# Seven-product steps: the first product's bank is copied into the fourth one's bank instead of being added afterwards

## The chip, the cores and the metric

The kernel runs on one core of one Trainium2 chip. What is measured is the device time of one execution in microseconds (us). The engines are TensorE (PE; its weight loads are listed as PEld), VectorE (DVE), ScalarE (ACT), GpSimd (POOL) and SyncE (SP), which issues most DMAs. A name such as L915 is a line of the kernel.

## The reference

Attention within chunks of 64 positions, and a gated feed-forward network on its result:

```python
scores = q_c @ k_c.T / sqrt(64)               # 8 batches, 8 heads, 9 chunks of 64, width 64
attn = softmax(scores)
x = (attn @ v_c) as (4608 tokens, 512)
g = x @ w_gate                                # 512 x 1536
out = (g * sigmoid(g)) * (x @ w_val) @ w_out  # 1536 x 512
```

All data are float32. The kernel splits each factor into an upper and a lower half in a shorter format and multiplies three pairs of halves, so every product below is made of three matmuls for each 128 rows of its inner dimension.

## The kernel before, in words

Tokens are worked on in batches of 512 (`N`), and the feed-forward network in twelve slices of 128 hidden columns (`f`, or a step). From slice 5 of the first batches on, gate and value of a slice are computed for two batches at once from seven products of half-size blocks in place of eight. Seven steps of this kind run in `first_seven` (L928; f = 5 to 11), and 36 in `gated_pair` (L1189), twelve for each of the three later pairs of batches (`both_steps`, L1256).

**A step.** Product i (`seventh`, L910 to L916; its matmuls are L915) takes six matmuls of 128x512 and adds into one of three PSUM banks. Bank `ps1` is from the pool `ps_a`; `ps2` and `ps3` are the two banks of the pool `ps_gv`. The order on TensorE is:

- products 0, 1 and 2 go to `ps1`, `ps2` and, added to what is there, `ps1`; after each of the first three ScalarE copies the bank to SBUF: the first copy (L953, L1202) to `h`, the second (L961, L1204) to `v2`, the third (L968, L1207) to `v1`;
- product 3 goes to `ps3`; VectorE adds it to `h` (`add`, L918; its instruction is L919), and ScalarE turns `h` into its Silu in place (L977, L1211);
- product 4 adds into `ps1`, and VectorE adds that bank to `v2`; product 5 adds into `ps2`, and VectorE adds that bank to `v1` and multiplies `h` by it (L555);
- product 6 adds into `ps1`, and ScalarE takes its Silu (L995, L1223), which VectorE multiplies by `v2`.

Between the products stand the four quarters (`turns`, L921) of the output projection of the step before: three matmuls each, L583 to L585 of 128x512 or L571 of 128x256. `parts` (L562) splits `h` for the next step's projection.

```python
seventh(ps1, pair.x, factors, 0, True)     # L1201
nc.scalar.copy(out=h, in_=ps1)             # L1202
...
seventh(ps3, pair.x, factors, 3, True)     # L1209
add(h, ps3)                                # L1210
nc.scalar.activation(h, h, AF.Silu, scale=2.0 ** -8)
```

**What else uses the banks.** `ps_gv` and `ps_a` also hold the attention's scores and outputs. In the steps 0, 3, 8 and 10 of a pair that is not the last, a burst of attention work for the next pair is put before the last quarter: `scores` (L1099) after steps 0 and 3, `cross` (L1118) after 8 and 10. In `scores` the second two banks of scores are in `ps_gv`; for each of them `less_top` (L318) takes a row maximum (L322) and subtracts it (L323) on VectorE. `cross` has its banks emptied by ScalarE (L398). The helpers `products` and `scores` (L292, L300) and `columns_crossed` (L386) write one bank with many 64x64 matmuls; in `products` and `columns_crossed` each of them has the flag `start`.

**What sets the order.** The order on TensorE, ScalarE and VectorE is the order of the program text throughout (L611). SyncE's is so until L1049 and GpSimd's from L1456 to L1559; in the pairs after that, from L1560, the order of those two is made when the program is built, from an estimated timeline. `load_weights` (L1181; its DMAs are L1186) loads the two tiles of factors of step i + 2 at the end of step i, into the place of step i's.

Of the kernel before, what the change touches and what calls it, by code (L numbers as in the profile page):

```python
# [13 lines left out]
AF = mybir.ActivationFunctionType  # L14
# [4 lines left out]
C = 64  # L19
# [14 lines left out]
def attn_then_gated_ffn(ctx: ExitStack, tc: tile.TileContext, qk, v, wgv, wo, out):  # L34
    nc = tc.nc
# [18 lines left out]
    def in_turn(x):  # L54

        return x.rearrange("p (a b) -> p b a", a=2)
# [158 lines left out]
    def save_w(f):  # L215
        kept_w[f] = store.tile([P, 2, 4 * Q], F32, name=f"w{f}")
        nc.sync.dma_start(out=kept_w[f], in_=w_both[f].bitcast(F32))
# [50 lines left out]
    class Attn:  # L268
# [23 lines left out]
        def products(self, tiles, pool=ps_a, tag="ps_a"):  # L292

            n = sum(t.shape[1] for t in tiles)
            ps = [pool.tile([P, n, T, C], F32, name="ps_a", tag=tag) for _ in range(2)]
            for i, t in enumerate(t[:, k] for t in tiles for k in range(t.shape[1])):
                self.scores(t, i, ps)
            return ps

        def scores(self, t, i, ps, first=None):  # L300
# [85 lines left out]
        def columns_crossed(self, v_t, p, n, pool=ps_a, tag="ps_a"):  # L386


            px = [pool.tile([P, n, T, C], F32, name="ps_a", tag=tag) for _ in range(2)]
            for i in range(n):  # L390
                for u in range(T):
                    for j in range(2):
                        for h in range(2):
                            r = (h ^ j) * C
                            nc.tensor.matmul(px[j][h * C:(h + 1) * C, i, u, :], v_t[i][r:r + C, j, u, :],  # L395
                                             self.turned[r:r + C, p + i, j, u, :], start=True, stop=True)
            for j in range(2):
                nc.scalar.copy(out=self.s[:, p:p + n, :, j], in_=px[j])  # L398

# [101 lines left out]
    def some(ps, a, f, g, which, first=True, last=True):  # L501
        for k, i in which:
            w = (w_hi, w_lo, w_hi)[i][f][:, g, k]
            x = a.x[k // 2][i == 0][:, k % 2]
            nc.tensor.matmul(ps, w, in_turn(x), start=first and (k, i) == which[0],  # L505
                             stop=last and (k, i) == which[-1])
# [12 lines left out]
    def save_o(f):  # L519
        nc.sync.dma_start(out=kept_o[f], in_=out_now[f].bitcast(F32))  # L520
        if f % 2 == 0:
            kept_raw.append(store.tile([P, 2, DM], F32, name=f"r{f}"))
        nc.sync.dma_start(out=kept_raw[f // 2][:, f % 2], in_=wo_raw[f])
# [14 lines left out]
    def product(a, f, g):  # L538
        ps = ps_gv.tile([P, N], F32, name="ps_gv")
        some(ps, a, f, g, IN_TURN)  # L540
        return ps
# [12 lines left out]
    def times(h, pv):  # L554
        nc.vector.scalar_tensor_tensor(out=h, in0=pv, scalar=2.0 ** -8, in1=h, op0=ALU.mult, op1=ALU.mult)  # L555

    def gated(a, f):
        h = gate(a, f)
        times(h, value(a, f))
        return h  # L560
# [57 lines left out]
    def put_off(h):  # L618
        f = len(waiting)
        if f % 2 == 0:  # L620
            kept_h.append(store.tile([P, 2, N], F32, name=f"h{f}"))
        waiting.append(kept_h[-1][:, f % 2])
        nc.scalar.dma_start(out=waiting[f], in_=h)
# [44 lines left out]
    class Product:  # L668
# [4 lines left out]
        def add(self, *which):  # L673
            for w in which:
                self.left -= 1
                some(self.ps, *self.at, [w], first=self.left == 3 * NK - 1, last=not self.left)
# [88 lines left out]
    for do in opening.split():  # L765
# [14 lines left out]
        else:  # L780
            b, i = int(do[1]), int(do[2])
# [128 lines left out]
    def seventh(ps, x, factors, i, first):  # L910
        which, q = FACTORS[i]
        w = [t.rearrange("p (i k m) -> p i k m", i=4, m=P)[:, q] for t in factors[which]]
        for k in range(NK // 2):
            for n, (u, v) in enumerate(((0, 1), (1, 0), (0, 0))):
                nc.tensor.matmul(ps, w[u][:, k], in_turn(x[i][v][:, k]), start=first and k == 0 and n == 0,  # L915
                                 stop=k == NK // 2 - 1 and n == 2, skip_group_check=True)  # L916
# [4 lines left out]
    def turns(which):  # L921

        if pending:
            project(*pending[0], which=which)
            if T - 1 in which:
                pending.pop()

    def first_seven(f, done, before, amid=None):  # L928

        o, w = down[f], up[f + 1] if f + 1 < NF else None  # L930
        if f + 2 < NF:
            up[f + 2].load()
        save_o(f - 1)
        done.save()
        if f == NF - 2:
            save_w(EARLY)
            save_w(EARLY + 1)
        factors = (w_both[f][:, 0], w_both[f][:, 1]), done.halves

        def product(ps, i, first):  # L940
            seventh(ps, x_first, factors, i, first)

        ps1 = ps_a.tile([P, N], F32, name="ps_a", tag="ps_a")
        ps2, ps3 = (ps_gv.tile([P, N], F32, name="ps_gv") for _ in range(2))
        h = hp.tile([P, N], F32, name="h")
        v1, v2 = (ld.tile([P, N], F32, name="v", tag="v_t") for _ in range(2))
        product(ps1, 0, True)
        if w:
            w.below()
            w.shift()  # L950
        if f + 1 < NF:
            down[f + 1].load()
        nc.scalar.copy(out=h, in_=ps1)  # L953
        o.below()
        if f < NF - 1:
            put_off(before)
        product(ps2, 1, True)
        if w:
            w.join()
            w.upper()  # L960
        nc.scalar.copy(out=v2, in_=ps2)  # L961
        turns([0])
        product(ps1, 2, False)
        quarters = Quarters(f + 1)
        if w:
            quarters.sums(w.t)
            w.lower()
        nc.scalar.copy(out=v1, in_=ps1)  # L968
        if w:
            quarters.upper()  # L970
        o.shift()
        o.join()
        product(ps3, 3, True)
        add(h, ps3)
        if w:
            quarters.lower()
        nc.scalar.activation(h, h, AF.Silu, scale=2.0 ** -8)  # L977
        turns([1])
        product(ps1, 4, False)
        add(v2, ps1)  # L980
        wo_f = out_weights(f, nc.gpsimd)
        product(ps2, 5, False)
        if f + 2 < NF:
            up[f + 2].scale()
        if f + 1 < NF:
            down[f + 1].scale()
        add(v1, ps2)
        times(h, v1)
        p = parts(a0, f, h)
        turns([2] if amid is None else [2, 3])  # L990
        if amid:
            amid()
        product(ps1, 6, False)
        h2 = const.tile([P, N], F32, name="h2", tag="ts") if f == NF - 2 else hp.tile([P, N], F32, name="h")
        nc.scalar.activation(h2, ps1, AF.Silu, scale=2.0 ** -8)  # L995
        if amid is None:
            turns([3])
        times(h2, v2)
        pending.append((p, wo_f))
        return quarters, h2  # L1000
# [188 lines left out]
    def gated_pair(pair, i, h, h2, inside, middle, beside):  # L1189

        def turn_of(t):
            if t in inside:
                turns([t])

        factors = loaded[STEPS[i]]
        ps1 = ps_a.tile([P, N], F32, name="ps_a", tag="ps_a")
        ps2 = ps_gv.tile([P, N], F32, name="ps_gv")
        ps3 = ps_gv.tile([P, N], F32, name="ps_gv")
        v12 = const.tile([P, 2, N], F32, name="v", tag=("ts", "wo1")[i % 2])
        v1, v2 = v12[:, 0], v12[:, 1]  # L1200
        seventh(ps1, pair.x, factors, 0, True)  # L1201
        nc.scalar.copy(out=h, in_=ps1)  # L1202
        seventh(ps2, pair.x, factors, 1, True)
        nc.scalar.copy(out=v2, in_=ps2)  # L1204
        turn_of(0)
        seventh(ps1, pair.x, factors, 2, False)
        nc.scalar.copy(out=v1, in_=ps1)  # L1207
        middle()
        seventh(ps3, pair.x, factors, 3, True)  # L1209
        add(h, ps3)  # L1210
        nc.scalar.activation(h, h, AF.Silu, scale=2.0 ** -8)  # L1211
        beside()
        turn_of(1)
        seventh(ps1, pair.x, factors, 4, False)
        add(v2, ps1)
        seventh(ps2, pair.x, factors, 5, False)
        add(v1, ps2)
        times(h, v1)
        if i == NF - 1:
            prepare_unit(pair, 0)  # L1220
        turn_of(2)
        seventh(ps1, pair.x, factors, 6, False)
        nc.scalar.activation(h2, ps1, AF.Silu, scale=2.0 ** -8)  # L1223
        times(h2, v2)
        turn_of(3)
        return parts(pair, i, h)
# [216 lines left out]
    a, pair = nxt, []  # L1443
# [29 lines left out]
    pair = pair[0]  # L1473
# [65 lines left out]
    for i in range(NF):  # L1539
        f = (i + EARLY) % NF  # L1540
        h = gated(a, f)
# [18 lines left out]
    for b in range(3, NB, 2):  # L1560
# [27 lines left out]
        if not pair.last:  # L1588
            pair = n
# [34 lines left out]
```

## Time and profile before

| | |
|---|---|
| median of 3 runs | 848.16 us |
| the three runs | 846.42, 848.16, 850.94 us |
| span of the profiled execution | 846.1 us |
| instructions | 16689 |
| TensorE busy | 828.3 us, 98% of the span |
| VectorE busy | 605.8 us, 72% |
| ScalarE busy | 433.5 us, 51% |
| GpSimd busy | 158.7 us, 19% |

The span is the time from the first to the last instruction of the profiled execution; the table of runs does not single that execution out, and the lowest of the three is 0.3 us above the span. A line of the timeline gives the start in us from the span's beginning, the duration in us, the engine, the line, the operation, what is written and read, and in brackets the idle time of the engine just before and what ended it. Successive matmuls overlap, so that the durations of single matmuls add up to more than the time they take together; starts are compared instead.

### The profile page before, as it was taken

The page shows a single profiled execution, that of the slowest core. Times are in us where ns is not written, and L with a number is a line of the kernel's source. Part 1 is how long each engine was busy: PE and PEld are TensorE (multiplying, and loading weights), DVE is VectorE, ACT ScalarE, POOL GpSimd, SP SyncE. Part 2 cuts the span into 40 slices and gives each one's busy share as a digit, 9 for nine tenths or more (in the row PEclk, how much of TensorE's full clock was granted, in tenths as well). Part 3 has the DMA queues.
Part 4 walks back from the last instruction along what each step waited for, and adds up shares of the span by engine and source line. Part 5 has one row for each costly group of instructions (what it writes and reads, how often), then busy time and mean ns, then how long its engine had stood idle before and what let it go on. Part 6 is the DMA issues. An engine that isn't in the chain of part 4 may idle for free.

```text
span 846.1 us, 16689 instructions
## 1 busy us (share of the span) xinstructions
PE 828.3 (98%) x6689; PEld 742.8 (88%) x6689; DVE 605.8 (72%) x946; ACT 433.5 (51%) x650; POOL 158.7 (19%) x118
## 2 busy tenths in 40 slices
PE   7999999999998999999999999999999999999997
PEld 6788888888887888888889998888889988888997
DVE  5898988863798965568886976688768943333475
ACT  5876889753525335535335744553337533333353
POOL 1300001102246641233110002313010002222100
PEclk9999999999999999999999999999999999999999
DMA  9698788899989999866678779656668576666643
GB/s 353 257 330 312 279 312 313 320 350 324 418 298 380 304 405 346 306 210 232 231 245 309 266 247 323 229 214 237 194 229 300 163 260 229 232 232 227 234 170 114
DMA packets 96654, 231.27 MB, mean 273 GB/s; under 512 B 32064, under 2 KB 58176, under 8 KB 83904
## 3 DMA queue, kind: packets, MB, share of 16 engines
q1 hardware_dynamic: 94848, 227.31, 75.1%
q10 hardware_dynamic: 1728, 2.88, 1.1%
q8 instruction: 53, 0.87, 0.4%
q14 instruction: 25, 0.20, 0.1%
HBM read 177.21 MB, written 52.95 MB: 272 GB/s over the span
## 4 chain that ended last, share of the span: by engine, by line
PE 86%; DMA 6%; DVE 3%; ACT 1%; SPq 1%; issue 1%; POOL 1%; DVEq 0%; POOLq 0%; ACTq 0%
PE ps_a L915 26%; PE ps_gv L915 19%; PE ps_o L571 14%; PE ps_gv L505 9%; PE ps_gv L571 6%; DMA v_t<-in_v 3%; PE ps_o L583 3%; PE ps_o L585 3%; PE ps_o L584 3%; DMA qk_t<-r 2%; PE ps_a L395 2%; PE ps_a L307 1%; DVE turned L382 1%; DMA both<-o 1%; DMA qk_t<-in_qk 1%
## 5 line engine op out<-in xcount | busy, mean ns | idle before, releaser
L915 PE MATMUL ps_a<-x,factors 128*128 128x512 f32 x864 | 210.7, 380 | 0.8 <-ACT v L1204 0.8
L915 PEld LDWEIGHTS ps_a<-x,factors 128*128 128x128 f32 x864 | 154.4, 190 | 18.1 <-issue 1.0
L915 PE MATMUL ps_gv<-x,factors 128*128 128x512 f32 x648 | 157.5, 379 | 0.1
L915 PEld LDWEIGHTS ps_gv<-x,factors 128*128 128x128 f32 x648 | 122.3, 189 | 17.9 <-PE ps_a L915 0.4
L1249 POOL TENSOR_TENSOR kept<-kept 128x512 f32<-128x512 f32 x39 | 56.9, 1459 | 365.3 <-DVE kept L555 361.0
L505 PE MATMUL ps_gv<-xh,w 128*128 128x512 f32 x352 | 103.4, 380 | 2.0 <-issue 2.0
L382 DVE STREAM_TRANSPOSE turned<-s_sb 32x256 f32<-32x256 f32 x192 | 83.7, 436 | 3.1
L70 ACT CAST hh<-kept 128x512 fp32r<-128x512 f32 x111 | 67.2, 617 | 28.8 <-PE ps_o L571 15.4
L505 PEld LDWEIGHTS ps_gv<-xh,w 128*128 128x128 f32 x352 | 66.4, 189 | 9.5 <-ACT xh L660 0.2
L1223 ACT ACTIVATE kept<-ps_a 128x512 f32<-128x512 f32 x36 | 21.5, 598 | 89.7 <-PE ps_a L915 89.3
L919 DVE TENSOR_TENSOR kept<-kept,ps_gv 128x512 f32<-128x512 f32 x30 | 20.6, 687 | 65.1 <-PE ps_gv L915 64.9
L71 DVE TENSOR_TENSOR hl<-kept,hh 128x512 fp32r<-128x512 f32 x84 | 57.2, 686 | 12.4 <-ACT hh L70 12.0
L505 PE MATMUL ps_gv<-xl,w 128*128 128x512 f32 x176 | 65.5, 382 | 0.0
L555 DVE SCALAR_TENSOR_TENSOR kept<-v,kept 128x512 f32<-128x512 f32 x66 | 45.7, 692 | 24.2 <-ACT kept L1223 18.0
L571 PE MATMUL ps_o<-sums,hh 128*128 128x256 f32 x504 | 62.7, 275 | 0.0
L571 PEld LDWEIGHTS ps_o<-sums,hh 128*128 128x128 f32 x504 | 59.3, 192 | 0.4 <-DVE hh L71 0.4
L571 PEld LDWEIGHTS ps_o<-both,hh 128*128 128x128 f32 x288 | 51.4, 189 | 6.8
L583 PE MATMUL ps_o<-both,hl 128*128 128x512 f32 x144 | 55.0, 382 | 0.8 <-DMA both<-o 0.8
L584 PE MATMUL ps_o<-both,hh 128*128 128x512 f32 x144 | 54.6, 379 | 0.0
L585 PE MATMUL ps_o<-both,hh 128*128 128x512 f32 x144 | 54.6, 379 | 0.0
L571 PE MATMUL ps_o<-both,hh 128*128 128x256 f32 x288 | 53.5, 276 | 0.0
L919 DVE TENSOR_TENSOR v<-v,ps_a 128x512 f32<-128x512 f32 x43 | 29.5, 686 | 22.0 <-PE ps_a L915 21.6
(164 smaller groups left out, 1442.4 us busy)
## 6 DMA issues: line engine op xcount, KB each, us to landing
factors<-w SPq DMA_DIRECT2D x36, 1024.0 KB, 4.9
factors<-t SPq DMA_DIRECT2D x36, 1024.0 KB, 6.9
sums<-sums SPq DMA_DIRECT2D x36, 512.0 KB, 5.9
w<-w SPq DMA_DIRECT2D x16, 1024.0 KB, 9.1
t<-th SPq DMA_DIRECT2D x24, 512.0 KB, 5.1
raw<-in_wgv SPq DMA_DIRECT2D x11, 1024.0 KB, 9.0
both<-o SPq DMA_DIRECT2D x22, 512.0 KB, 9.1
qk_t<-in_qk SPq DMA_DIRECT2D x10, 1024.0 KB, 11.0
```

What stands on the lines that cost most here:

```text
L70: nc.scalar.copy(out=hi, in_=src)
L71: (engine or nc.vector).tensor_tensor(out=lo, in0=src, in1=hi.bitcast(F32), op=ALU.subtract)
L382: nc.vector.transpose(out=self.turned[to:to + 32, p:p + 2, j, :, 32 * (i % 2):32 * (i % 2) + 32], in_=src[32 * i:32 * i + 32, :, o // 2, 3 ...
L505: nc.tensor.matmul(ps, w, in_turn(x), start=first and (k, i) == which[0], stop=last and (k, i) == which[-1])
L555: nc.vector.scalar_tensor_tensor(out=h, in0=pv, scalar=2.0 ** -8, in1=h, op0=ALU.mult, op1=ALU.mult)
L571: nc.tensor.matmul(banks[t // 2][:, t % 2], h[u][:, t * P:(t + 1) * P], in_turn(w[v]), start=first and t % 2 == 0 and n == 0, stop=n == 2, ...
L583: nc.tensor.matmul(o, hl[:, ts], woh, start=f == a.steps[0], stop=False)
L584: nc.tensor.matmul(o, hh[:, ts], wol, start=False, stop=False)
L585: nc.tensor.matmul(o, hh[:, ts], woh, start=False, stop=f == a.steps[1])
L915: nc.tensor.matmul(ps, w[u][:, k], in_turn(x[i][v][:, k]), start=first and k == 0 and n == 0, stop=k == NK // 2 - 1 and n == 2, skip_group ...
L919: nc.vector.tensor_tensor(out=t, in0=t, in1=ps, op=ALU.add)
L1249: engine.tensor_tensor(out=out, in0=one, in1=two, op=op)
```

## The change

ScalarE copies the first product's bank not into `h` in SBUF but into `ps3`. Product 3 then adds into that bank, VectorE's addition of `ps3` to `h` is left out, and the Silu reads `ps3` and writes `h`. In the bursts that share these banks the flag `start` is now set only on the first matmul in each bank and half of the partitions.

```diff
@@ products
-                self.scores(t, i, ps)
+                self.scores(t, i, ps, i == 0)
@@ columns_crossed
-                                             self.turned[r:r + C, p + i, j, u, :], start=True, stop=True)
+                                             self.turned[r:r + C, p + i, j, u, :], start=(i, u) == (0, 0), stop=True,
+                                             skip_group_check=True)
@@ first_seven
-        nc.scalar.copy(out=h, in_=ps1)
+        nc.scalar.copy(out=ps3, in_=ps1)
...
-        product(ps3, 3, True)
-        add(h, ps3)
+        product(ps3, 3, False)
         if w:
             quarters.lower()
-        nc.scalar.activation(h, h, AF.Silu, scale=2.0 ** -8)
+        nc.scalar.activation(h, ps3, AF.Silu, scale=2.0 ** -8)
@@ gated_pair
         seventh(ps1, pair.x, factors, 0, True)
-        nc.scalar.copy(out=h, in_=ps1)
+        nc.scalar.copy(out=ps3, in_=ps1)
...
         middle()
-        seventh(ps3, pair.x, factors, 3, True)
-        add(h, ps3)
-        nc.scalar.activation(h, h, AF.Silu, scale=2.0 ** -8)
+        seventh(ps3, pair.x, factors, 3, False)
+        nc.scalar.activation(h, ps3, AF.Silu, scale=2.0 ** -8)
```

## Rows read from the trace of the kernel before

**Rows 1.** The head of the page.
```profile
span 846.1 us, 16689 instructions
```

**Rows 2.** Busy time by stage: stretch, its length, busy us (instructions) by engine, clock, DMA.
```profile
322.00:458.00 136.00, 136.00 (x1164) 120.87 (x1163) 97.12 (x162) 60.40 (x96) 29.24 (x19) 1.00 0.74 258
```

**Rows 3.** Waits of TensorE: what waited, for what, us in total, times, longest.
```profile
PE ps_gv L505 <- issue: 2.0, 1, 2.0
...
PE ps_a L395 <- issue: 1.2, 1, 1.2
...
PE ps_a L915 <- ACT v L1204: 0.8, 1, 0.8
PE ps_a L495 <- issue: 0.7, 1, 0.7
...
PE ps_a L915 <- DVE v L919: 0.3, 1, 0.3
```

**Rows 4.** Groups of VectorE: busy us, mean ns, idle before and what ended it.
```profile
L919 DVE TENSOR_TENSOR kept<-kept,ps_gv 128x512 f32<-128x512 f32 x30 | 20.6, 687 | 65.1 <-PE ps_gv L915 64.9
```

**Rows 5.** Groups of ScalarE, same columns.
```profile
L70 ACT CAST x<-s_sb 128x1024 fp32r<-128x1024 f32 x15 | 15.4, 1049 | 0.0
...
L88 ACT ACTIVATE t<-raw 128x1024 f32<-128x1024 f32 x11 | 16.7, 1521 | 0.0
...
L1202 ACT COPY kept<-ps_a 128x512 f32<-128x512 f32 x30 | 17.6, 588 | 23.9 <-PE ps_a L915 23.9
```

**Rows 6.** Timeline, an ordinary step of the first pair.
```profile
381.40 1.46 PE L915 MATMUL ps_gv<-x,factors 128*128 128x512 f32 x6
381.60 0.59 ACT L1202 COPY kept<-ps_a 128x512 f32<-128x512 f32 x1 [0.53 <-PE ps_a L915]
...
383.03 1.46 PE L915 MATMUL ps_a<-x,factors 128*128 128x512 f32 x6
...
384.33 1.46 PE L915 MATMUL ps_gv<-x,factors 128*128 128x512 f32 x6
...
390.37 0.32 SPq L1186 DMA_DIRECT2D factors<-t  x1
```

**Rows 7.** The DMAs of line 1186, the loads of factors: issue to landing.
```profile
DMA to landing us min/median/max: 4.6/6.3/12.1
```

**Rows 8.** Timeline, the first step of the first stage of seven products.
```profile
102.36 0.68 DVE L919 TENSOR_TENSOR h<-h,ps_gv 128x512 f32<-128x512 f32 x1
...
102.96 1.22 DVE L177 TENSOR_TENSOR th<-ts,th 128x1024 fp32r<-128x1024 f32 x1
...
104.10 0.68 DVE L919 TENSOR_TENSOR v<-v,ps_a 128x512 f32<-128x512 f32 x1
...
104.18 0.38 PE L585 MATMUL ps_o<-both,hh 128*128 128x512 f32 x1
...
104.83 0.48 PE L915 MATMUL ps_a<-xl,th 128*128 128x512 f32 x1 [0.27 <-DVE v L919]
```

**Rows 9.** Timeline, the steps after the four bursts of scores.
```profile
337.60 0.69 DVE L323 TENSOR_TENSOR s_sb<-ps_a,top 128x512 f32<-128x512 f32 x1
...
339.11 1.46 PE L915 MATMUL ps_a<-x,factors 128*128 128x512 f32 x6
...
371.42 0.69 DVE L323 TENSOR_TENSOR s_sb<-ps_a,top 128x512 f32<-128x512 f32 x1
...
372.62 1.46 PE L915 MATMUL ps_a<-x,factors 128*128 128x512 f32 x6
...
513.86 0.69 DVE L323 TENSOR_TENSOR s_sb<-ps_a,top 128x512 f32<-128x512 f32 x1
...
515.03 1.46 PE L915 MATMUL ps_a<-x,factors 128*128 128x512 f32 x6
...
547.35 0.69 DVE L323 TENSOR_TENSOR s_sb<-ps_a,top 128x512 f32<-128x512 f32 x1
...
548.55 1.46 PE L915 MATMUL ps_a<-x,factors 128*128 128x512 f32 x6
```

## Prediction

> **What bounds the kernel now.** I read the page's head first, for the span, and then the busy time by stage. In the 136 us in which the first pair of batches runs its twelve steps, TensorE is busy for all 136.00 us [rows 1, 2]. So these steps are TensorE's own time, and work taken off VectorE shortens them only where TensorE stands and waits for VectorE. Third, the waits of TensorE: the reader is to look for the lines of the seven products (L915) and for what ended each wait. There are two, 0.8 us put down to ScalarE and 0.3 us put down to VectorE [rows 3]. Three further waits have no releaser that the profile shows and are outside these steps (2.0, 1.2 and 0.7 us). Last, the order of time inside one step [rows 6]: product 1 starts at 381.40, product 2 at 383.03 with a quarter turn between them, product 3 at 384.33. A product takes 1.30 us, a product with a quarter turn 1.63, so a step of seven products and four quarter turns takes 3 x 1.30 + 4 x 1.63 = 10.42 us, with no room between its parts.
>
> **Removed: VectorE's addition.** Each of the 43 steps (7 in `first_seven`, 36 in `gated_pair`) loses one addition of 0.687 us [rows 4], 29.5 us of VectorE in all. What waits for it is only ScalarE's Silu, whose result is wanted after two more products. The cover is TensorE's unbroken work, so I cost it at nothing, with one exception. In the first step of the first stage (f = 5) the addition at 102.36 stands ahead of a 1.22 us pass at 102.96, and that stands ahead of the addition for v2 at 104.10, which reads the bank that product 6 writes [rows 8]. That addition ends at 104.78 and product 6 starts at 104.83, after L585's matmul at 104.18. One sixth of 1.30 is 0.22, so it should start at 104.40: 0.43 lost, and 0.10 more because the first matmul after the stop takes 0.48 instead of 0.38. With the addition of 102.36 gone the long pass ends 0.6 us sooner, v2's addition ends before 104.40, and what is late next is nothing: **-0.53 us**.
>
> **Moved: the Silu.** It waits for TensorE's fourth product instead of VectorE and reads PSUM instead of SBUF. It starts about 0.7 us sooner; behind it on ScalarE stands the Silu of product 6, which waits for TensorE anyway. Nothing on TensorE's path, so 0. That product 3 now adds into the bank instead of writing it afresh changes no length: products 2 and 3 are one of each kind and both show 1.46 us in the timeline [rows 6]. The other flags that the diff touches change neither the number nor the order of matmuls: 0.
>
> **Changed: the copy's destination.** The copy takes 0.588 us into SBUF [rows 5]. No row shows ScalarE writing PSUM. The lower end is a copy so short that no step waits for it; the upper end is the 1.05 us of a ScalarE cast over 1024 columns, as if reading and writing the same memory had to take turns [rows 5]. I take 0.59, the nearest row, the same operation and shape. In an ordinary step the copy runs from 381.60 to 382.19 and product 2, which must not add to the bank before it is read, starts at 383.03 [rows 6]. The handover costs some 0.05 (104.78 to 104.83 above), so there are 0.79 us to spare, and neither 0.59 nor 1.05 costs anything there.
>
> The Trainium skill (ScalarE: Activation LUTs, Step-by-step: what each stage is for) says that ScalarE writes PSUM faster than SBUF; no run here shows it yet. It gives some 93 ns of overhead for ScalarE on SBUF and 51 on PSUM elsewhere (Perfetto Trace Analysis, Optimizing Scalar/DVE Operations): by these, an estimate, the copy would take 0.55, and the sum below would be 0.1 us lower.
>
> **Added: a wait for the fourth bank.** The copy needs that bank free early in the step; before, it was first touched two products later. Its last reader is usually ScalarE's own Silu of the step before, in order. But after the two bursts of scores of a pair (steps 0 and 3, in two pairs), VectorE's subtraction L323 reads that bank last, while the next step is already running. Behind the waiting copy on ScalarE stands v2's copy, which has three products of room; for the copy itself waits product 2. Worked out with 0.05 for each handover, 0.59 for the copy and 0.10 for the restart [rows 9]:
> - 371.42 + 0.69 = 372.11 free; copy 372.16 to 372.75; product 2 at 372.80, not 372.62: 0.18 + 0.10 = 0.28.
> - 513.86 + 0.69 = 514.55; copy to 515.19; 515.24, not 515.03: 0.31.
> - 547.35 + 0.69 = 548.04; copy to 548.68; 548.73, not 548.55: 0.28.
> - 337.60 + 0.69 = 338.29; copy to 338.93; 338.98, before 339.11: 0.
>
> Together **+0.87 us**. With a copy of 1.05 each is 0.46 later: 0.74, 0.77, 0.74 and, for the fourth, 0.33 + 0.10 = 0.43, so 2.68; with the lower end 0.
>
> The Trainium skill (Perfetto Trace Analysis, Matmuls) speaks against such a hold: groups of matmuls should rotate through banks, so that one is emptied beside the next. The rows say the same at the three places above and nowhere else.
>
> **Sum.** 846.1 - 0.53 + 0.87 = 846.4 us for the profiled execution, with ends 845.6 (no wait at all) and 846.1 - 0.53 + 2.68 = 848.3. The page gives this execution a span of 846.1; the median of the three runs is 848.16, 2.1 above it, so I add the difference of +0.3 to the median: **848.5 us**, ends 847.6 and 850.3. The change is worth nothing measurable: half a per cent, 4.2 us, is about what a measurement of this kernel can tell from no change.
>
> **Rivals.**
> - *The copy into PSUM is slow, and every step pays (slower).* It decides from 0.59 + 0.79 = 1.38 us on. At 1.52, a far ScalarE row [rows 5], 39 steps lose 0.14 + 0.10 = 0.24 each, 9.4 us, and the four after bursts 1.21, 1.24, 1.21 and 0.90, 4.6 us: 846.1 - 0.5 + 14.0 = 859.6, or 861.7 against the median. For it: no row shows a write from ScalarE to PSUM. Against: ScalarE's copies out of PSUM take no longer than half of this.
> - *A load comes late (slower).* In the pairs the order of SyncE and GpSimd is not written by hand but made from an estimated timeline when the program is built, so other durations can move loads past each other. A step's second load of factors is issued at 390.37 [rows 6] for a product 1 two steps after that of 381.40, at 402.24: 11.9 us, of which landing takes 6.3 in the median [rows 7], so 5.6 to spare. Held back by a whole step, 10.4, it stops TensorE for 4.8: 851.2, or 853.3 against the median, for one such load. Against: before, no product waits for a load, with the same kind of order.
> - *Gaps that belong to the program's layout go (faster).* The three waits for nothing shown, and the 0.8 us put down to a ScalarE copy, make 2.0 + 1.2 + 0.7 + 0.8 = 4.7 [rows 3]. Without them 846.4 - 4.7 = 841.7, or 843.8. For it: the change removes instructions and so shifts the programs. Against: TensorE's own list stays as long as it was.
>
> **How the numbers follow.** Forecast 0.85 (with up to one gap more or less), slow copy 0.03, late load 0.06, gaps 0.06. The three readings of the unchanged kernel reach from 846.42 to 850.94, so the range takes the ends 847.6 and 850.3, a spread of 1.2 to 2.6 below for repeats and gaps that go in part, and 1.2 above: 845.0 to 851.5. That leaves out the rivals' own times and little of the forecast. Faster by over 0.5%: 0.06, the gaps. Slower: 0.03 + 0.06 = 0.09, less one part for a late load that is half hidden: 0.08. Within: 0.86.
>
> **What would show it.** VectorE busy 29 us less, with 43 additions gone; the copy near 0.59 into the fourth bank; TensorE still busy for all of the first pair's steps; the wait before product 6 at 104.83 gone; product 2 waiting for the copy after three of four bursts, by about 0.3 us, and product 3 never. A copy above 1.05 us, a product waiting in most steps, or a load of factors ahead of a wait of TensorE would make the prediction wrong; so would a drop of several us with these waits unchanged.

## Result and the profile after

The changed kernel takes 856.11 us in the median of six runs (855.35 to 856.65), the kernel before 848.05, also in six; the ratio is 1.0095, interval 1.0079 to 1.0112. It is slower by 0.95%, and 4.6 us above the upper end of my range.

The head of the changed kernel's page: span, then busy us, share and instructions of TensorE and VectorE, and the queue by which TensorE's list of instructions is loaded (loads, MB, share).

```profile
span 854.9 us, 16679 instructions
PE 831.0 (97%) x6689; PEld 744.2 (87%) x6689; DVE 577.6 (68%) x903; ACT 432.6 (51%) x650; POOL 160.4 (19%) x118
...
q8 instruction: 53, 0.87, 0.4%
```

The span is 8.8 us longer than before [rows 1] with the same 6689 matmuls. VectorE has the 43 additions less. The edit did what it says, and TensorE waits longer. Its waits, longest in total first (us in total, times, longest):

```profile
PE ps_gv L916 <- issue: 5.6, 4, 2.1
PE ps_a L395 <- issue: 2.9, 1, 2.9
...
PE ps_o L584 <- DMA both<-o: 1.8, 1, 1.8
...
PE ps_a L496 <- issue: 1.2, 1, 1.2
...
PE ps_o L572 <- issue: 0.8, 1, 0.8
PE ps_gv L916 <- PE ps_a L916: 0.8, 1, 0.8
PE ps_gv L916 <- ACT t L96: 0.7, 1, 0.7
```

L916 is the products' line here (L915 before). In [rows 3] a product waited twice, 1.1 us together, and both were products into `ps_a`. Now six waits stand before products into `ps_gv`, 7.1 us of idle time, and the two of [rows 3] are gone. Five of the six are waits for a bank; the sixth, of 2.1 us, is one of the gaps below. The timeline tells where: the first step, two of the four steps after bursts of scores, and an ordinary step.

```profile
95.64 0.68 DVE L556 SCALAR_TENSOR_TENSOR h<-ps_gv,h 128x512 f32<-128x512 f32 x1
...
96.31 0.58 ACT L954 COPY ps_gv<-ps_a 128x512 f32<-128x512 f32 x1
...
96.47 1.53 PE L916 MATMUL ps_gv<-x,th 128*128 128x512 f32 x6 [0.74 <-ACT t L96]
...
372.73 1.46 PE L916 MATMUL ps_a<-x,factors 128*128 128x512 f32 x6
...
374.27 0.57 ACT L1202 COPY ps_gv<-ps_a 128x512 f32<-128x512 f32 x1 [1.73 <-PE ps_a L916]
374.45 0.69 DVE L323 TENSOR_TENSOR s_sb<-ps_a,top 128x512 f32<-128x512 f32 x1
...
375.24 1.53 PE L916 MATMUL ps_gv<-x,factors 128*128 128x512 f32 x6 [1.05 <-issue]
...
385.72 1.46 PE L916 MATMUL ps_gv<-x,factors 128*128 128x512 f32 x6
385.98 0.57 ACT L1202 COPY ps_gv<-ps_a 128x512 f32<-128x512 f32 x1 [0.58 <-PE ps_a L916]
...
387.35 1.46 PE L916 MATMUL ps_a<-x,factors 128*128 128x512 f32 x6
...
516.72 1.56 PE L916 MATMUL ps_a<-x,factors 128*128 128x512 f32 x6
...
518.36 0.57 ACT L1202 COPY ps_gv<-ps_a 128x512 f32<-128x512 f32 x1 [1.34 <-PE ps_a L916]
518.88 0.69 DVE L323 TENSOR_TENSOR s_sb<-ps_a,top 128x512 f32<-128x512 f32 x1
...
519.67 1.53 PE L916 MATMUL ps_gv<-x,factors 128*128 128x512 f32 x6 [1.39 <-issue]
```

The reader is to see which product waits. After the burst, product 0 starts at 372.73 and product 1 would follow 1.30 us later, at 374.03; it starts at 375.24, 0.10 after the end of the *second* subtraction L323 (374.45 + 0.69). The copy, which I had waiting for that bank, starts at 374.27, before that subtraction itself has begun. So the two have changed places: the copy has the bank that is free first, product 1 the one that VectorE empties last. The same stands at 519.67 (end of L323: 519.57) and in the first step, where product 1 starts 0.15 after VectorE's L556 has left its bank at 96.32. The profile puts this wait down to ScalarE's L96, which ends at nearly the same time; e9 below, in which only the banks of these steps change places, takes it away. By starts, the five waits are 0.90, 0.92, 1.22, 1.55 and 1.22 us, 5.8 together, of which 0.23 were there before. Ordinary steps lose nothing: from product 1 to product 2 at 385.72 and 387.35 are 1.63 us, as in [rows 6].

The kernel is 8.06 us slower in the medians; the bank waits are 5.6 of it, and 0.5 was gained in the first step (below), so about 3 us are left. Part of them are gaps for which the profile names nothing ("issue"). Before, they are 2.0, 1.2 and 0.7, and 0.8 that was put down to a copy [rows 3], 4.7 together. After, they are 2.9, 1.2, 0.8 and one of 2.1, which the first of the rows above counts with the products' waits, 7.0 together. Three of them:

```profile
265.77 0.30 PE L395 MATMUL ps_a<-turned,v_t 64*64 64x64 f32 x1 [2.94 <-issue]
266.00 0.79 PE L506 MATMUL ps_gv<-xl,w 128*128 128x512 f32 x1
266.59 1.06 PE L506 MATMUL ps_gv<-xh,w 128*128 128x512 f32 x2
...
432.05 0.38 PE L572 MATMUL ps_o<-both,hh 128*128 128x256 f32 x1 [0.84 <-issue]
...
611.59 1.13 PE L916 MATMUL ps_gv<-x,factors 128*128 128x512 f32 x4 [2.12 <-issue]
```

The first of these gaps has a tail. The windows view of the stretch behind it (length, busy us of each engine, granted clock, DMA share, GB/s):

```profile
265.70:269.20 3.50, 3.42 (x9) 2.69 (x10) 2.31 (x2) 1.53 (x2) 0.79 (x1) 0.53 1.04 385
```

The granted clock is 0.53 of full speed, near its lower level of 1.2 GHz, after TensorE had been idle for 2.94 us; three matmuls in a row that span 0.43 from first start to last at full speed span 0.85 here (266.59 to 267.44), which costs some 1.5 us more.

In the two profiled executions, compared matmul by matmul, this adds up: 5.6 for the banks, less 0.5, 2.3 for the gaps, 1.5 for the slow matmuls, and 1.0 for a wait for a load of output weights (`both`), 1.8 us where it was 0.8, make 9.9; some 1.1 was gained in small waits of the first 260 us, and 8.8 is the difference of the spans. The wait for the load is not taken for the change's doing: it is 1.6 in e4, which has none of the bank changes and the time of the kernel before.

### The profile page after: what moved, and what is told of

Same layout as the page of the kernel before. It is cut to its first block, busy times and chain, and to the rows that moved or that the text cites. A ratio compares the mean times of both kernels' runs of the same rounds, so it can differ in the third digit from the quotient of the medians.

```text
span 854.9 us, 16679 instructions
## 1 busy us (share of the span) xinstructions
PE 831.0 (97%) x6689; PEld 744.2 (87%) x6689; DVE 577.6 (68%) x903; ACT 432.6 (51%) x650; POOL 160.4 (19%) x118
## 4 chain that ended last, share of the span: by engine, by line
PE 89%; DMA 4%; DVE 2%; issue 2%; ACT 1%; SPq 1%; POOL 0%; DVEq 0%; POOLq 0%; ACTq 0%
PE ps_a L916 26%; PE ps_gv L916 20%; PE ps_o L572 14%; PE ps_gv L506 10%; PE ps_gv L572 6%; PE ps_o L584 3%; PE ps_o L586 3%; PE ps_o L585 3%; DMA qk_t<-r 2%; DMA qk_t<-in_qk 2%; PE ps_a L395 1%; PE ps_a L307 1%; DVE turned L382 1%; PE ps_a L496 1%; DMA both<-o 1%
## 5 line engine op out<-in xcount | busy, mean ns | idle before, releaser
L916 PE MATMUL ps_a<-x,factors 128*128 128x512 f32 x864 | 210.2, 380 | 0.0
L916 PEld LDWEIGHTS ps_a<-x,factors 128*128 128x128 f32 x864 | 154.3, 190 | 16.8
L916 PE MATMUL ps_gv<-x,factors 128*128 128x512 f32 x648 | 158.1, 380 | 6.4 <-issue 5.6
L916 PEld LDWEIGHTS ps_gv<-x,factors 128*128 128x128 f32 x648 | 122.1, 189 | 25.4 <-issue 7.1
L572 PE MATMUL ps_o<-sums,hh 128*128 128x256 f32 x504 | 62.7, 275 | 0.0
L556 DVE SCALAR_TENSOR_TENSOR kept<-v,kept 128x512 f32<-128x512 f32 x66 | 45.7, 693 | 23.4 <-ACT kept L1222 17.2
L572 PEld LDWEIGHTS ps_o<-sums,hh 128*128 128x128 f32 x504 | 59.3, 192 | 0.4 <-DVE hh L71 0.4
L572 PEld LDWEIGHTS ps_o<-both,hh 128*128 128x128 f32 x288 | 51.4, 189 | 8.0 <-issue 1.1
L572 PE MATMUL ps_o<-both,hh 128*128 128x256 f32 x288 | 53.8, 276 | 0.8 <-issue 0.8
L920 DVE TENSOR_TENSOR v<-v,ps_gv 128x512 f32<-128x512 f32 x43 | 29.6, 688 | 25.7 <-PE ps_gv L916 25.7
```

Source lines behind the costliest of these rows:

```text
L572: nc.tensor.matmul(banks[t // 2][:, t % 2], h[u][:, t * P:(t + 1) * P], in_turn(w[v]), start=first and t % 2 == 0 and n == 0, stop=n == 2, ...
L920: nc.vector.tensor_tensor(out=t, in0=t, in1=ps, op=ALU.add)
```

## Experiments

Theory A: banks; product 1 now takes the one that is emptied last, and waits for it. Theory B: the hold of the bank, or the copy into it, costs something in every step. Theory C: part of the loss are gaps beside loads of TensorE's list of instructions, and what stands at these gaps moves when the list gets longer or shorter. Each kernel was timed in five rounds with the kernel before on the same chip; the ratio to it counts, because the kernel before came to 846.95 to 847.58 us there.

| | median us | ratio to before |
|---|---|---|
| the change | 856.11 | 1.0095 (1.0079 to 1.0112) |
| e1, copy written after product 1 | 848.00 | 1.0008 (0.9994 to 1.0021) |
| e2, before, other bank last | 846.60 | 0.9988 (0.9976 to 1.0000) |
| e3, change, other bank last | 853.22 | 1.0065 (1.0050 to 1.0080) |
| e4, flags alone | 847.82 | 1.0004 (0.9992 to 1.0016) |
| e5, change, list 12 shorter | 852.80 | 1.0062 (1.0042 to 1.0083) |
| e6, e1, list 12 shorter | 849.15 | 1.0017 (1.0005 to 1.0029) |
| e7, before, list 12 shorter | 847.01 | 1.0004 (0.9992 to 1.0016) |
| e8, e1 and ScalarE empties | 847.11 | 0.9999 (0.9986 to 1.0011) |
| e9, e1 in first seven steps only | 851.82 | 1.0049 (1.0031 to 1.0066) |
| e10, e1 in the pairs only | 848.56 | 1.0015 (1.0001 to 1.0029) |
| e11, e8, list 12 shorter | 846.99 | 0.9993 (0.9979 to 1.0007) |
| e12, e8, list 6 shorter | 847.00 | 0.9990 (0.9973 to 1.0007) |

**e1: the copy written after product 1.**

```diff
@@ gated_pair (and the same in first_seven)
-        nc.scalar.copy(out=ps3, in_=ps1)
         seventh(ps2, pair.x, factors, 1, True)
+        nc.scalar.copy(out=ps3, in_=ps1)
         nc.scalar.copy(out=v2, in_=ps2)
```

> The changed kernel, with the copy into the fourth bank written after product 1 in the text; the order on every engine stays, only the bank that each gets changes. Theory A (banks): in the changed kernel the copy gets the bank of ps_gv that is free first and product 1 the one that VectorE empties last, so product 1 waits after the four bursts and at the first step (0.92, 1.22, 1.55, 1.22 and 0.90 us). Here product 1 gets the first bank again and only the copy waits: these waits fall to about 0.3 us or less before product 2, and the time falls by 4 to 5 us, to 851 or 852. Theory B (the hold or the copy itself costs something in every step): nothing changes, 856. Theory C (gaps with no releaser, which move with the instruction list): 856 give or take 2, with the five waits still there.

The slowdown is gone: 1.0008. The order of work on TensorE, VectorE and ScalarE is what it was; moving one line of text (in `first_seven`, past two further calls as well) changed only who takes which bank and who waits for what. Its timeline at two places after bursts:

```profile
369.84 1.46 PE L916 MATMUL ps_gv<-x,factors 128*128 128x512 f32 x6
370.27 0.69 DVE L323 TENSOR_TENSOR s_sb<-ps_a,top 128x512 f32<-128x512 f32 x1
...
371.07 0.57 ACT L1203 COPY ps_gv<-ps_a 128x512 f32<-128x512 f32 x1 [2.71 <-DVE s_sb L323]
...
371.69 1.56 PE L916 MATMUL ps_a<-x,factors 128*128 128x512 f32 x6
...
512.36 1.53 PE L916 MATMUL ps_gv<-x,factors 128*128 128x512 f32 x6
512.89 0.69 DVE L323 TENSOR_TENSOR s_sb<-ps_a,top 128x512 f32<-128x512 f32 x1
...
513.67 0.57 ACT L1203 COPY ps_gv<-ps_a 128x512 f32<-128x512 f32 x1 [2.63 <-DVE s_sb L323]
...
514.29 1.56 PE L916 MATMUL ps_a<-x,factors 128*128 128x512 f32 x6
```

Here the copy waits for the subtraction (370.96, copy at 371.07) and product 2 for the copy, 0.22 us and 0.10 of restart (the first matmul after a stop takes that much longer), while product 1 has started before the subtraction. This is the schedule that I had worked out for the change itself. Theory B falls: the hold is there in all 43 steps and costs nothing that the trace shows outside three of them. The gain is larger than the 4 to 5 us of theory A alone.

**e2 and e3: the other bank emptied last**, in the kernel before and in the changed one.

```diff
@@ less_top
-            for h in range(2):
+            for h in (1, 0):
```

> The kernel before, with VectorE emptying the second bank of scores first and the first one last, in every use of less_top of the pairs; nothing else. Theory A: product 1, which takes the first bank, waits about 1 us after each of the four bursts, the time rises by 4 to 5 us, to 852 or 853, without any of the change in it. Theory B: 848, as before. Theory C: 848 give or take 2, no new waits of product 1.

> The changed kernel, with the same reversal. Theory A: product 1, which here takes the second bank, finds it empty in time, so the four waits after bursts go and the copy waits instead; product 2 then waits 0.3 us at most. The wait of 0.90 in the first step stays. The time falls by 3.5 to 4.5 us, to about 852. Theory B and C: 856 give or take 2.

Both expectations missed on the point they were made for. First e2, then e3, at the burst before 512 us:

```profile
510.41 0.69 DVE L323 TENSOR_TENSOR s_sb<-ps_a,top 128x512 f32<-128x512 f32 x1
...
511.20 1.53 PE L915 MATMUL ps_gv<-x,factors 128*128 128x512 f32 x6
...
511.73 0.69 DVE L323 TENSOR_TENSOR s_sb<-ps_a,top 128x512 f32<-128x512 f32 x1
```

```profile
516.05 0.57 ACT L1202 COPY ps_gv<-ps_a 128x512 f32<-128x512 f32 x1 [1.35 <-DVE s_sb L323]
516.60 0.69 DVE L323 TENSOR_TENSOR s_sb<-ps_a,top 128x512 f32<-128x512 f32 x1
...
517.39 1.53 PE L916 MATMUL ps_gv<-x,factors 128*128 128x512 f32 x6 [1.43 <-issue]
```

In e2 product 1 still starts 0.10 after the first subtraction, in e3 still 0.10 after the second. So a bank is not bound to a tile: of the two tiles of this pool in a step, the one that is written first in the text gets the bank that is emptied first, whichever that is. (The tiles themselves are declared in the same order, `ps2` and then `ps3`, in all five kernels.) The bank numbers of the built programs say the same. At the burst after step 0 the scores are emptied from 0 and then 1 (from 1 and then 0 in e2 and e3); product 1 has 0 before, 1 in the change, 0 in e1, 1 in e2 and 0 in e3, and the copy has the other one in each changed kernel. At the burst after step 3 some of the numbers are swapped, and who gets the bank emptied first is the same. Theory A stands with this correction. That e3 is nevertheless 0.3% under the change while its five waits are the same (0.90 to 1.60 by starts) is for the gaps: the one that was 2.94 us is 2.58 there, without slow matmuls behind it, and the one of 2.12 is 1.48.

**e4: the flags alone**, the first two hunks of the change on the kernel before.

> The kernel before with the flags of the 64x64 matmuls alone changed as in the diff. All theories: 848, no wait new; if the flags cost something, the L307 and L395 bursts would take longer than 2.1 us each.

They cost nothing that can be measured: 1.0004.

**e5, e6, e7: TensorE's list 12 instructions shorter** ahead of everything, on the change, on e1 and on the kernel before. The left-out transposes are read by nobody.

```diff
-    keep_warm(15)
+    keep_warm(9)
```

> The changed kernel with 6 of the 15 warm-up transposes at the very start left out (nothing reads them), so that TensorE's list of instructions is 12 shorter ahead of everything else. Theory C (part of the loss are gaps beside instruction loads, which stand at fixed places of the list; the changed kernel has 7 more waits on TensorE's list by the gap at 265 us and 15 more by that at 611): the gaps at matmuls 2247, 3511 and 5026 (3.2, 1.0 and 2.3 us) shrink to at most 2.1, 0.3 and 1.0, the five waits of product 1 stay, and the time falls by 2 to 4 us to 852 to 854. Theory A alone (banks are all of it): the start may save up to 1 us, 855 to 856, the gaps as before.

> The kernel of e1 (copy written after product 1) with the same 6 transposes left out. Theory C: its gaps (1.8, 2.0 and 1.4 us at matmuls 2250, 2502 and 5027) shrink, the time falls by 1 to 3 us below e1, to 845 to 847. Theory A alone: 847 to 848.

> The kernel before with the same 6 transposes left out: the control for the start. Theory C: the start and smaller gaps (2.1, 1.4 and 0.95 before) save 1 to 3 us, 844 to 847. Theory A alone: 847 to 848.

e5 is 0.33% under the change, 2.8 us, while the control e7 gains nothing. TensorE's waits in e5:

```profile
PE ps_gv L916 <- issue: 3.5, 3, 1.4
...
PE ps_a L395 <- issue: 1.4, 1, 1.4
...
PE ps_o L572 <- issue: 0.9, 1, 0.9
PE ps_gv L916 <- PE ps_a L916: 0.8, 1, 0.8
PE ps_gv L916 <- ACT t L96: 0.7, 1, 0.7
```

The bank waits are all there (3.5 in the row that had 5.6, and the 0.8 and 0.7). The gaps have moved. The burst that was cut at 265.77 now runs through:

```profile
262.29 2.11 PE L395 MATMUL ps_a<-turned,v_t 64*64 64x64 f32 x128
```

The 1.4 at L395 is another gap, at 298.96, where the kernel before has its 1.2. The gap of 0.8 at 432.05 is gone, and the 0.9 at L572 is the one of 2.1 at 611.59, six matmuls further on in the text and shorter. The two intervals overlap a little (e5 up to 1.0083, the change from 1.0079), so that the 2.8 us are not certain to the last part. e6 missed: expected 1 to 3 us below e1, it is 0.1% above it, no more than the intervals allow, with one gap of 2.9 at L395. Shifting the list moves gaps and does not always shorten them.

Where the change has more on its list than e1 is seen in the wait instructions of the products' line, in the change and then in e1 (how many, durations in ns, first and last start in us):

```profile
L916 PEldq EVENT_SEMAPHORE  x52: 51/51/3071, 96.4 to 796.5; - x52
```

```profile
L916 PEldq EVENT_SEMAPHORE  x51: 51/51/1747, 317.3 to 787.7; - x51
```

In the change they begin at 96.4, in e1 at 317.3. In the first seven steps one matmul, the first of product 1, has to wait for VectorE's bank and for ScalarE's factors, and a second wait is an instruction of its own: by the trace, 7 more on TensorE's list ahead of the gap at 265 us than in e1 (48 and 41; 41 in the kernel before, too). Over the whole span the change has 189 wait instructions on TensorE's list, e1 188 and the kernel before 163: e1's list is as long as the change's in the end, and e1 loses nothing.

**e9 and e10: the order of e1 in one of the two functions.**

> The changed kernel with the copy written after product 1 in the first seven steps only. Theory A: the wait of 0.90 us in the first step goes, the four waits after bursts stay: 855. Theory A with C: besides, TensorE's list loses its 7 extra waits ahead of the attention stage, as product 1 there no longer waits for two engines in one matmul, so the gap at matmul 2247 (3.2 us and slow matmuls behind it) falls to about 2: together 1.5 to 3.5 us less than the changed kernel, about 853 to 854.5.

> The changed kernel with the copy written after product 1 in the 36 steps of the pairs only. Theory A: the four waits after bursts (0.92, 1.22, 1.55, 1.22) go, three of 0.2 before product 2 and one of 0.2 before product 1 come: 4 us less, 852. Theory A with C: the same 4 us, and the wait of 0.90 and the gap of about 3 us at matmul 2247 stay as they are: 851 to 853.

The first seven steps alone take back 0.46% (3.9 us), where the wait itself is 0.9; the pairs alone 0.80% (6.8 us), where I expected 4; both together 0.87% (7.4 us). The parts do not add up, as they would if each were its waits alone, though by little more than the four intervals allow. In e10 the wait of the first step is still there, and so is a gap at L395, but shorter:

```profile
PE ps_a L395 <- issue: 1.7, 1, 1.7
...
PE ps_gv L916 <- ACT t L96: 0.7, 1, 0.7
```

The list up to that gap is as long in e10 as in the change, 48 wait instructions by the trace, and yet the gap is 1.7 and not 2.9. So the length of the list is not all that sets it.

The traces say more of these gaps. Counted as weight loads, matmuls, wait instructions and the one drain at the start, 4544 instructions of TensorE's list stand ahead of the gap that ends at 264.63 in the kernel before, and 4545 ahead of the one that ends at 265.77 in the change; that is 17 x 256 and 192 or 193 more. In the fourteen traces there are 48 gaps of 0.3 us or more at places 192 or 193 past a multiple of 256, at five such places in all, and each ends 1.2 to 1.6 us after a load of 16 KB of TensorE's list has ended. Every gap of that size put down to "issue" is among them, except the products' waits for banks. So 7 waits more ahead of such a place put it three matmuls earlier in the text, and 12 instructions fewer put it six later. How long TensorE stands there goes with the start of the load: before 264.63 it starts at 262.31, 0.36 us ahead of TensorE's stop, and before 265.77 at 263.51, 0.68 us behind it. What decides when the load starts stays open.

**e8, e11, e12: a version below both?** e1, and in the bursts ScalarE copies all four banks of scores to SBUF, so that none of them waits for VectorE; e11 and e12 are e8 with 9 and 12 warm-up transposes in place of 15.

```diff
@@ scores, beside_pair
-            a.less_top(ps[1], 2)
+            a.less_top(a.take(ps[1], 2), 2)
```

> The kernel of e1, and in the bursts of scores ScalarE copies also the two banks of ps_gv to SBUF, from where VectorE takes the maximum; both banks are then free before product 1. The waits of product 2 after bursts (0.2 us each, three) and that of product 1 at 512 us (0.2) go: 0.7 to 1 us less than e1 by theory A; by theory C this is lost in gaps that move, 847 to 849.

> The kernel of e8 (copy after product 1, ScalarE empties the scores) with 6 warm-up transposes left out, to look for a version under the kernel before. Theory A alone: as e8, 847. Theory C: its gaps at matmuls 2250, 3514 and 5029 (1.9, 0.7, 1.3) shrink and one at 2502 may grow: 845 to 848.

> The same with 3 transposes left out, a list 6 shorter. Theory A alone: 847. Theory C: gaps between those of e8 and of e11, 844 to 847.

All three intervals hold 1. The waits after the bursts are gone, and the time is that of the kernel before: no version beats it by more than a measurement of this size can tell.

## Why the prediction was wrong, point by point

- **The addition's removal**: right. 28 us less VectorE work, and the only wait that I can put down to it is the one of [rows 8]: product 6 of the first step now follows its quarter turn without a stop, worth 0.5 us.
- **The moved Silu and the flags**: right, nothing (e4: 1.0004).
- **The copy's price**: right within its bounds. The copy into PSUM takes 0.57 us in all 36 steps of the pairs, 0.02 less than into SBUF [rows 5]. The Trainium skill (ScalarE: Activation LUTs, Step-by-step: what each stage is for) has the direction right, by 0.02 us here; the 0.55 worked out from the Trainium skill's overheads (Perfetto Trace Analysis, Optimizing Scalar/DVE Operations) was too low. The slow-copy rival falls with it.
- **"Added: a wait for the fourth bank"**: this is the step that failed. I took it that the copy would get the bank that product 3 had, and product 1 keep its own. The bank goes by whose write comes first in the text, so the wait fell to product 1, which has no room, in place of the copy, which has 0.8 us. The term was +0.87 and measured 5.6 (0.90 + 0.92 + 1.22 + 1.55 + 1.22, less 0.23 that was there). The 0.90 of it stand in the first step, where I had no wait at all: there too VectorE, and not ScalarE's Silu, reads the bank last. With the banks as I had them in mind (e1), the term is right: 0.22 and 0.10 of restart at three of four places, and a ratio of 1.0008 (0.9994 to 1.0021) where +0.3 us is 1.0004.
- **The gaps**: the second thing that went wrong. The rival had them only go, and argued that TensorE's own list stays as long as it was. The matmuls do stay, but 26 wait instructions came in (163 and 189). The gaps grew by 2.3 us, and the slow matmuls behind one of them cost 1.5 more; the range had 1.2 us above for repeats and gaps together. That the gaps stand at fixed places of the list, beside its loads, is in all fourteen traces. The way from more waits to longer gaps is not shown: e10 has as many ahead of the gap at L395 and stands 1.7 us there in place of 2.9, and e6, with fewer, has a gap of 2.9 at another place.
- **The late load** of factors did not come: no product of the changed kernel waits for one. (The longer wait for output weights, 1.8 us, is before a quarter turn, and e4 has one like it.)

## What to carry to other kernels

When an instruction is made to write a buffer earlier, ask not only whether that buffer is free, but which buffer it now takes from the pool and what is left for the work that used to come first. Where two takers of a rotating pool stand close together, let the one with no room write first in the text; here this cost one moved line and was worth 0.9%. And a time difference of a few us on an engine that is busy 97% of the span may lie in gaps that have nothing to do with the arithmetic: compare the same matmul's gap in both traces before giving it to the change.

## What was not expected of the hardware

- TensorE stands still for 0.3 to 3 us at a few places where no semaphore is late, inside a burst of 64x64 matmuls or within some 3 us behind one, always 192 or 193 instructions past a multiple of 256 on its list, with a load of the kind "instruction" just before (one of 16 KB from 609.1 to 610.0 us, before the gap that ends at 611.59). The Trainium skill (Runtime: NRT & Kernel Launch, Instruction fetch mechanics) says that an engine's list comes in blocks of 16 KiB, 256 instructions each, and that crossing into the next one is mostly hidden. The 53 loads of 0.87 MB and the places of the gaps agree with the block. Four of the change's crossings are not hidden, at 1.2, 2.9, 0.8 and 2.1 us; at the others no gap of 0.3 us stands. A burst of 128 matmuls and their 128 weight loads, 256 instructions, is done in about 2.1 us. That the loads are the cause is argued from place and time in all fourteen traces; no run changed the loads alone.
- After 2.94 us of such idle time the granted clock was 0.53 for the next 3.5 us; after 1.96 us in the kernel before it stayed at 1.00, and after 2.58 us in e3 too. In e5 it was 0.62 over 4.5 us after a wait of 1.99 us for a load (257.8 to 262.3). So the length of the stop alone does not tell whether the clock falls.
